# Sliding-window attention in blocks of 32 queries by 64 keys instead of 64 by 96, in a fused attention and mixture-of-experts kernel

## The chip, the core and the metric

The kernel runs on one core of a Trainium2 chip. The metric is the device time of one execution in microseconds (us). The kernel before takes 619.64 us, the median of three runs (619.24 to 620.0). "TensorE" is the matmul engine (PE in the profile, PEld its weight loads), "VectorE" is DVE, "ScalarE" ACT, "GpSimd" POOL, and SP issues most loads.

## The reference

Attention with a local window, then two feed-forward layers, all in fp32:

```python
q, k, v: (2, 8, 576, 64)            # batch, heads, positions, head size
rel = pos[:, None] - pos[None, :]
mask_plain = (rel >= 0) & (rel < 32)                      # heads 0 to 3
mask_dil = (rel >= 0) & (rel < 128) & (rel % 4 == 0)      # heads 4 to 7
scores = where(mask, q @ k.T / 8, -1e9)
attn = exp(scores - max); attn = attn / (attn.sum(-1) + 1e-9)
x = (attn @ v), heads side by side                        # (1152, 512)
p = domain_probs / (domain_probs.sum(-1) + 1e-9)
x = sum over 4 experts e of p[:, e] * (relu(x @ w1[e]) @ w2[e])   # 512 -> 1024 -> 512
h = x @ w_in                                              # 512 -> 2048
out = (h - tanh(h)) @ w_out
```

Each query sees 32 keys: in a plain head its own position and the 31 before it, in a dilated head every fourth position back. A dilated head is four plain windows over positions of equal remainder by 4.

## The kernel before

The 1152 tokens are worked in two sets: set 0 has the first 512, set 1 the other 640 (`SETS`). The feed-forward products ("dense products" below) are in fp32r, each value split into a high and a low part (`split`, line 761), so that every product is three matmuls; from the third weight slice on, a seven-product scheme (`PROD`, `product`) saves one product in eight. They stream 512, 320 or 256 columns.

Attention is worked in blocks of `BQ` = 64 queries by `BK` = 96 keys (64 and a halo of 32). Host code (`_pack`) lays q, k and v out by `PARTS`. The tensors q and k lie with the head size on the partitions, two heads above each other (a = 0, 1), and pairs of heads c = 0, 1. For set 0, class `Piece` works in two halves of 256 tokens, for the plain and the dilated heads; for set 1, class `Pair` works four times, once per kind and pair of heads.

1. Scores (lines 1096 and 1241): fp32 products with 64 partitions (head size) and 64 queries as weights, streaming 96 keys. They stand in a PSUM bank as stacks: 128 partitions (two blocks of 64 queries) by 96 columns per stack, four or five stacks in a bank.
2. Mask: in set 0 a bf16 product of an identity with a stored mask opens the bank, and the scores add to it (`open`, line 1230). In set 1 VectorE adds a stored mask (`masked`, line 1118).
3. Softmax (lines 1124 and 1278): maximum on VectorE, exponential on ScalarE, sum, reciprocal, and the division as a product on GpSimd. `STYLE` chooses, for a bank, one exponential per stack with its sum (0) or one for all (1).
4. Transposes (line 1155): TensorE turns each stack of 128 x 96 into 96 x 128, and ScalarE copies the bank to SBUF.
5. Value products (lines 1190 and 1319): v as weights (96 keys on the partitions, 64 columns), 64 queries streamed, two heads into the two halves of a bank's partitions. The result is x, which ScalarE copies out.

The short last blocks of the dilated heads of set 1 (16 positions) are 32 queries wide and have a stack of their own (`load_v_short`, `last`).

The order of all instructions is made by a planner, class `Order`: operations are recorded with assumed costs and dependencies, then laid out engine by engine. TensorE goes through a list; operations marked `fill` may be pulled forward into waits, and `idle` fillers (`warm`, products of zeros) are dropped where there is nothing to fill. `first_attention` (line 1770) writes the list for set 0, `when` gives due times for set 1. Loads go on SP's queue in the planned order, the first k pieces on ScalarE's.

All instructions are recorded through one helper, so the profile gives line 340 for nearly all; rows are told apart by their tiles: `x,x` are scores, `ident,att` transposes, `w,h`, `att,h` and `att,x` with 64 columns as weights are value products, `p` masks, `zero` fillers, and 128 x 128 forms of `x,w` and `w,h` dense products.

Of the kernel before, what the change touches and what calls it, by code (L numbers as in the profile page):

```python
# [25 lines left out]
BQ = 64  # L26
# [13 lines left out]
]  # L40
OF = {(0, True): [0], (0, False): [1, 2], (1, True): [3, 4], (1, False): [5, 6, 7, 8]}


def blocks(W, plain):

    M = BQ if plain else W
    return W * DIL // M, M, M + HALO


def _halves():  # L50

    out, at = [], [0, 0, 0]
    for part, plain in PARTS:
        out.append((part, plain, tuple(at)))
        nb, M, K = blocks(part[2], plain)
        at[0] += 2 * nb * M
        at[1] += 2 * ((nb - 1) * (M if plain else K) + K)
        at[2] += nb * 4 * HEAD
    return out, at
# [160 lines left out]
class Program:  # L220
# [69 lines left out]
    def group(self):  # L290
        return _Group(self)
# [6 lines left out]
def _joined(found):  # L298

    if len(found) < 4:  # L300
        return list(found)
    plain = [r for r in found]
    return [(
        min(r[0] for r in plain), max(r[1] for r in plain),
        min(r[2] for r in plain), max(r[3] for r in plain), None,
    )]


class _Group:

    def __init__(self, program):
        self.program = program

    def __enter__(self):
        self.program.open = [0.0, [], [], []]
# [8 lines left out]
class Engine:  # L324
# [22 lines left out]
    def cost(self, method, kw, outs, ins):  # L347
        n = math.prod(outs[0].shape[1:])
        psum = any(v.tile.ring.psum for v in (*outs, *ins))
        if self.name == "tensor":  # L350
# [3 lines left out]
            if kw["lhsT"].dtype == F32:  # L354
                return 0.055 if n == 96 else 0.071, False
# [3 lines left out]
        if self.name == "scalar":  # L359
            if "accum_out" in kw:  # L360
                return 0.335 if any(v.tile.ring.psum for v in ins) else 0.39, False
# [317 lines left out]
def tile_local_attention_moe_tanhshrink(  # L679
# [97 lines left out]
    NST = {0: 4, 1: 5}  # L777
    masks, spare = {}, {}
    for g in range(2):
        for p in (True, False)[:1 + g]:  # L780
            t = Tile(p_r, [128, 640], BF16, loose=True).view()
            masks[g, p], spare[g, p] = t[:, :NST[g] * BK], t[:, NST[g] * BK:]
    ident_bf = spare[0, True][:, :128]
# [6 lines left out]
    m_ = {}  # L790

    def cols(m, j, n, p=slice(0, 128)):
        return m[p, j * BK:(j + n) * BK].rearrange("p (n w) -> p n w", w=BK)

    def wide(m, n, p=slice(0, 128)):
        return m[p].unsqueeze(1).to_broadcast([p.stop - p.start, n, BK])

    def emit_consts():

        m = masks[0, True]  # L800
# [1188 lines left out]
```

## Time and profile before

| | |
|---|---|
| median of 3 runs | 619.64 us |
| profiled execution | 619.3 us, span 617.5 us |
| TensorE matmul, busy | 612.9 us (99%) |
| VectorE, ScalarE, GpSimd, busy | 375.2, 307.8, 317.7 us (61%, 50%, 51%) |
| chain that ended last | TensorE 98% |
| TensorE's granted clock | 0.999 of full speed |
| mean load and store rate | 110 GB/s, over 300 GB/s in the first 45 us |

The span is the time from the first to the last instruction; the execution's own time has 1.8 us more around it. Ends of matmuls are modelled, so neighbouring rows overlap; distances between starts are read instead where it matters. A row of the trace merges instructions of a kind: the start, the time to the last end, and the count.

### The profile page before, as it was taken

How to read it: one execution, taken by the hardware profiler on the slowest of the kernel's cores; microseconds unless marked ns; L12 is line 12 of the kernel's file. 1: busy time of each engine (PE TensorE's matmuls, PEld its weight loads, DVE VectorE, ACT ScalarE, POOL GpSimd, SP SyncE). 2: the span in 40 equal slices, each digit the busy share in tenths (PEclk: the TensorE clock that was granted, in tenths of full speed). 3: DMA queues.
4: the chain of work that ended last, by engine and by line, in shares of the span. 5: the costliest groups of instructions: out<-in, count | busy, mean ns of one | idle time of the engine just before them, and what ended most of it. 6: DMA issues, size and time to landing. Idle time of an engine off the chain costs nothing.

```text
span 617.5 us, 10655 instructions
## 1 busy us (share of the span) xinstructions
PE 612.9 (99%) x4034; PEld 542.4 (88%) x4034; DVE 375.2 (61%) x726; ACT 307.8 (50%) x743; POOL 317.7 (51%) x281
## 2 busy tenths in 40 slices
PE   9999999999999999999999999999999999999998
PEld 5887798989889889889889889898898988988986
DVE  5764566867766767755425454547786676653652
ACT  7886675654434434424314355344766553652440
POOL 4779873754345335335425459764755663461220
PEclk9999999999999999999999999999999999999999
DMA  8993144172444455312112112333105424300012
GB/s 303 359 323 108 36 135 124 52 243 98 139 138 167 137 176 181 103 69 69 35 34 69 35 34 70 124 94 111 66 1 171 120 86 136 103 2 1 17 52 85
DMA packets 37554, 68.03 MB, mean 110 GB/s; under 512 B 4224, under 2 KB 12032, under 8 KB 37504
## 3 DMA queue, kind: packets, MB, share of 16 engines
q1 hardware_dynamic: 37216, 67.07, 33.4%
q8 instruction: 31, 0.51, 0.3%
q10 hardware_dynamic: 288, 0.30, 0.2%
q14 instruction: 19, 0.16, 0.1%
HBM read 56.61 MB, written 10.75 MB: 109 GB/s over the span
## 4 chain that ended last, share of the span: by engine, by line
PE 98%; DVE 1%; ACT 0%; POOL 0%; issue 0%; DVEq 0%; POOLq 0%; ACTq 0%
PE bank L340 98%; DVE x L340 0%; ACT att L340 0%; DVE bank L340 0%; DVE st L340 0%; POOL att L340 0%; DVE acc L340 0%; DVE att L340 0%; DVE h L340 0%; DVE zero L340 0%; DVEq L340 0%; POOLq L340 0%; ACTq L340 0%
## 5 line engine op out<-in xcount | busy, mean ns | idle before, releaser
L340 PE MATMUL bank<-w,h 128*128 128x512 f32 (+2 forms) x1404 | 323.5, 383 | 0.0
L340 PE MATMUL bank<-x,w 128*128 128x256 f32 (+2 forms) x1992 | 287.7, 299 | 0.4 <-DVE bank L340 0.4
L340 PEld LDWEIGHTS bank<-x,w 128*128 128x128 f32 x1992 | 277.8, 188 | 10.8 <-DVE bank L340 0.6
L340 PEld LDWEIGHTS bank<-w,h 128*128 128x128 f32 (+1 forms) x1404 | 241.4, 185 | 49.7 <-ACT w L340 1.0
L340 POOL TENSOR_TENSOR w<-raw,w 128x512 fp32r<-128x512 f32 x102 | 135.8, 1343 | 144.8 <-ACT w L340 143.3
L340 ACT ACTIVATE h<-bank 128x320 fp32r<-128x320 f32 (+4 forms) x168 | 69.0, 422 | 79.7 <-PE bank L340 65.7
L340 DVE SCALAR_TENSOR_TENSOR acc<-bank,pn,acc 128x512 f32<-128x512 f32 x59 | 44.2, 750 | 74.6 <-PE bank L340 74.6
L340 DVE TENSOR_TENSOR bank<-bank,p 128x320 f32<-128x320 f32 (+1 forms) x132 | 61.3, 467 | 37.1 <-PE bank L340 24.1
L340 DVE SCALAR_TENSOR_TENSOR h<-bank,h 128x320 fp32r<-128x320 f32 (+2 forms) x124 | 56.1, 464 | 35.3 <-ACT h L340 34.4
L340 ACT ACTIVATE w<-raw 128x512 fp32r<-128x512 f32 x108 | 67.5, 628 | 18.0 <-PE bank L340 15.6
L340 DVE SCALAR_TENSOR_TENSOR att<-att 128x512 int32<-128x512 int32 (+1 forms) x96 | 73.1, 777 | 1.3
L340 ACT ACTIVATE p<-bank 128x320 f32<-128x320 f32 (+1 forms) x88 | 36.3, 413 | 63.6 <-PE bank L340 62.8
L340 POOL TENSOR_TENSOR w<-sum,w 128x512 fp32r<-128x512 f32 x36 | 47.6, 1322 | 38.3 <-ACT w L340 38.2
L340 ACT ACTIVATE att<-bank 128x256 f32<-128x256 f32 (+3 forms) x78 | 32.2, 430 | 50.1 <-PE bank L340 42.5
L340 DVE TENSOR_TENSOR acc<-bank,acc 128x512 f32<-128x512 f32 (+1 forms) x28 | 18.8, 671 | 34.4 <-PE bank L340 34.3
L340 POOL TENSOR_TENSOR h<-att,h 128x256 fp32r<-128x256 f32 (+1 forms) x28 | 22.8, 835 | 26.8 <-ACT h L340 26.1
L340 ACT ACTIVATE att<-att 128x512 f32<-128x512 f32 (+2 forms) x39 | 25.3, 658 | 22.7 <-DVE att L340 16.9
L340 ACT ACTIVATE w<-sum 128x512 fp32r<-128x512 f32 x36 | 22.6, 628 | 20.5 <-PE bank L340 19.7
L340 POOL TENSOR_TENSOR sum<-raw 128x512 f32<-128x512 f32 x12 | 16.1, 1341 | 31.9 <-DMA raw<-in_moe_w_dram 17.8
L340 POOL TENSOR_TENSOR att<-att,st 128x480 f32<-128x480 f32 (+1 forms) x20 | 19.1, 956 | 14.2 <-DVE st L340 11.6
L340 DVE TENSOR_TENSOR bank<-bank,att 128x256 f32<-128x256 f32 (+1 forms) x32 | 14.8, 463 | 9.4 <-ACT att L340 9.1
L340 ACT ACTIVATE acc<-bank 128x512 f32<-128x512 f32 (+4 forms) x27 | 12.9, 505 | 11.7 <-PE bank L340 11.2
(73 smaller groups left out, 352.6 us busy)
## 6 DMA issues: line engine op xcount, KB each, us to landing
raw<-in_moe_w_dram SPq DMA_DIRECT2D x40, 512.0 KB, 3.9
att<-in_moe_w_in_dram SPq DMA_DIRECT2D x16, 512.0 KB, 5.0
att<-in_moe_w_out_dram SPq DMA_DIRECT2D x16, 512.0 KB, 4.9
in<-att SPq DMA_DIRECT2D x16, 256.0 KB, 3.8
out<-att SPq DMA_DIRECT2D x16, 256.0 KB, 3.3
raw<-in SPq DMA_DIRECT2D x8, 512.0 KB, 4.2
raw<-out SPq DMA_DIRECT2D x8, 512.0 KB, 3.7
h<-in_v_dram SPq DMA_DIRECT2D x7, 512.0 KB, 7.4
```

What stands on the lines that cost most here:

```text
L340: getattr(self.engine, method)(**real)
```

## The change

Blocks become 32 queries by 64 keys (`BQ` = 32). A score product has 32 query columns as weights and streams 64 keys; four blocks of 32 stand above each other and the two heads' rows of the array are used at once, so there are eight places in the array for it. A stack is 128 x 64, two stacks (s = 0, 1) are turned by one transpose of 128 x 128, and afterwards their keys lie on partitions 0 to 63 and 64 to 127. Value products are 64 keys deep and stream 32 queries; the two stacks use the two halves of the partitions and go to two banks, the two heads to the halves of a bank. So v is loaded with 128 partitions, the rows of one block above those of another. `Pair` and `Piece` become `Part` and `Early`: one softmax bank now holds both pairs of heads. Masks are made on TensorE from a small 64-row tile (`near`, `pick_`, `mask_in`). Rows of tokens in set 0 come in another order, which `y_sum` undoes. Planned costs and due times change with it.

The diff, cut to its core:

```diff
-BQ = 64
+BQ = 32
 BK = BQ + HALO
...
+    def mask_in(b, p, n, first):
+        m = 2 * first * BK
+        with P.group():
+            for to, x in ((b[:, :m], near), (b[:, m:n * BK], near[:, BK:])):
+                if to.shape[1]:
+                    w = x.shape[1]
+                    pe.matmul(
+                        out=to.rearrange("p (n w) -> p n w", w=w), lhsT=pick_[p],
+                        rhs=x.unsqueeze(1).to_broadcast([64, to.shape[1] // w, w]),
+                        start=True, stop=False, skip_group_check=True,
+                    )
...
     def emit_masks():
-        std, first = m_["std"], m_["first"]
...
+        for p in (True, False):
+            b = bank()
+            mask_in(b, p, 6, 2 if p else 1)
+            copy(masks[p], b[:, :6 * BK])
...
-            nb, M, K, n, at = self.parts[0]
-            o = c * nb * M + half * 256
-            load(self.q[:, o:o + 256], q[:, at[0] + o:at[0] + o + 256])
-            a, b = (0, 3 * M + K) if half == 0 else (3 * M + K, n)
-            load(self.k[c][:, a:b], k[:, at[1] + c * n + a:at[1] + c * n + b], queue)
+        def load_piece(self, c, u, queue="sync"):
+            at = HALVES[0][2]
+            for to, src, n in (
+                (self.home()[:, 512 * u + 256 * c:512 * u + 256 * c + 256], q[:, at[0] + 512 * c + 128 * u:], 128),
+                (self.home(c)[:, 320 * u:320 * u + 320], k[:, at[1] + 544 * c + 128 * u:], 160),
+            ):
+                load(
+                    to.rearrange("p (n w) -> p n w", n=2),
+                    src[:, :512].rearrange("p (n w) -> p n w", n=2)[:, :, :n],
+                    queue if n == 160 else "sync",
+                )
...
         def load_k_half(self, u):
-            t = self.k[u] = plain32(x_tile(self.g))
-            _, _, _, n, at = self.parts[u]
+            at, n = (HALVES[5][2][1], 1024) if u == 0 else (HALVES[4][2][1], 512)
...
+        def scores(self, c=None):
...
                     for a in range(2):
+                        r = slice(D * a, D * a + D)
+                        o = (2 * j + s) * BK
                         pe.matmul(
-                            out=self.sb[a][part:part + qs.shape[1], j * BK:(j + 1) * BK],
-                            lhsT=qs[D * a:D * a + D, :], rhs=ks[D * a:D * a + D, :],
-                            start=True, stop=True,
+                            out=self.sb[a][BQ * i:BQ * i + BQ, o:o + BK],
+                            lhsT=self.h.q[r, qo:qo + BQ], rhs=self.h.k[kt][r, ko:ko + BK],
+                            start=not opened_, stop=True, skip_group_check=True,
                         )
...
+            n = self.n * BK
             with P.group():
-                for j in range(4):
+                for j in range(0, n, 128):
                     pe.transpose(
-                        out=pb[:BK, j * 128:(j + 1) * 128], in_=t[:, 0, j * BK:(j + 1) * BK],
-                        identity=ident,
+                        out=pb[:, j:j + 128], in_=t[:, 0, j:j + 128], identity=ident,
                     )
...
+            banks = [bank() for _ in range(2)]
...
+                for j, s, i, i0, n, vt, vo, c, o, step in self.valued:
+                    rows = slice(64 * s, 64 * s + 64)
+                    w = j * 128 + BQ * i + i0
                     for a in range(2):
-                        f0 = j * 4 * D + (2 * self.c + a) * D
...
+                        f0 = vo * 4 * D + (2 * c + a) * D
+                        to = banks[s][D * a:D * a + D]
...
                         pe.matmul(
-                            out=to, lhsT=h.v[tile_][:BK, f0:f0 + D], rhs=w, start=True, stop=True,
+                            out=to, lhsT=h.v[vt][rows, f0:f0 + D], rhs=self.pt[a][rows, w:w + n],
+                            start=True, stop=True, skip_group_check=True,
                         )
```

How TensorE's list moves. Its beginning before, from the last filler ahead of the first scores (`zero` are fillers, `p` is the mask tile, `x,x` are scores):

```order
L340 LDWEIGHTS zero
L340 MATMUL bank<-zero 32x512
L340 LDWEIGHTS p
L340 MATMUL bank<-p 128x384
L340 MATMUL bank<-x_71,x_69 64x96 x8
```

Five more fillers stand ahead of these rows. The beginning now, from the first row:

```order
L362 LDWEIGHTS p
L362 MATMUL bank<-p 128x256
L362 LDWEIGHTS p
L362 MATMUL bank<-p 128x128
...
L362 LDWEIGHTS zero
L362 MATMUL bank<-zero 32x512
...
L362 MATMUL bank<-x_69,x_67 32x64 x16
L362 MATMUL bank<-x_83,x_67 32x64 x16
```

The list begins with masks, one filler is left ahead of the scores, and both pairs of heads are scored in a row.

TensorE's list around the first dense product, before (`x,w` is dense, `w,h` with 64 x 64 are values):

```order
L340 MATMUL bank<-ident,att 96x128 x4
L340 MATMUL bank<-w_311,h_176 64x64 x8
L340 LDWEIGHTS zero
L340 MATMUL bank<-zero 32x512
L340 MATMUL bank<-w_311,h_176 64x64 x8
L340 LDWEIGHTS p
L340 MATMUL bank<-p 128x384
L340 LDWEIGHTS p
L340 MATMUL bank<-p 128x384
L340 MATMUL bank<-x_327,w_331 128x256
```

And now:

```order
L362 MATMUL bank<-w_247,h_172 64x32 x32
L362 LDWEIGHTS p
L362 MATMUL bank<-p 128x256
L362 LDWEIGHTS p
L362 MATMUL bank<-p 128x256
L362 MATMUL bank<-ident,att 128x128 x4
L362 MATMUL bank<-x_396,w_390 128x256
L362 MATMUL bank<-x_433,w_390 128x256
```

All 32 value products of the first dilated half stand in one group, and four transposes of the second half have come ahead of the first dense product.

## Rows read from the trace of the kernel before

**Rows 1.** The page, part 4: the chain that ended last, by engine.

```profile
PE 98%; DVE 1%; ACT 0%; POOL 0%; issue 0%; DVEq 0%; POOLq 0%; ACTq 0%
```

**Rows 2.** The chain in order of time: start us, us, what.

```profile
9.32 443.19 PE bank L340 x3022
...
457.26 157.28 PE bank L340 x906
```

**Rows 3.** TensorE's groups, 16.42 to 103 us: shapes xcount | busy us, mean ns.

```profile
L340 PE MATMUL bank<-w,h 128*128 128x512 f32 x136 | 35.1, 402 | 0.0
L340 PE MATMUL bank<-x,w 128*128 128x256 f32 x180 | 24.5, 287 | 0.0
L340 PE MATMUL bank<-x,w 128*128 128x512 f32 x48 | 12.1, 401 | 0.0
```

**Rows 4.** TensorE's timeline, dense products alone: start us, us, what, count.

```profile
117.96 2.95 PE L340 MATMUL bank<-w,h 128*128 128x512 f32 x12
120.75 0.87 PE L340 MATMUL bank<-x,w 128*128 128x256 f32 x6
121.46 2.95 PE L340 MATMUL bank<-w,h 128*128 128x512 f32 x12
```

**Rows 5.** The same, scores and values with dense products beside them.

```profile
17.36 0.56 PE L340 MATMUL bank<-x,x 64*64 64x96 f32 x16
...
29.82 1.15 PE L340 MATMUL bank<-att,h 96*64 96x64 f32 x32
...
33.80 2.99 PE L340 MATMUL bank<-x,w 128*128 128x256 f32 x24
36.73 1.06 PE L340 MATMUL bank<-x,x 64*64 64x96 f32 x40
37.71 3.10 PE L340 MATMUL bank<-x,w 128*128 128x256 f32 x24
40.65 1.56 PE L340 MATMUL bank<-w,h 128*128 128x512 f32 x6
...
63.93 0.80 PE L340 MATMUL bank<-att,h 96*64 96x64 f32 x20
```

**Rows 6.** The same, transposes among dense products.

```profile
53.00 0.60 PE L340 MATMUL bank<-ident,att 128*96 128x128 f32 x4
53.35 3.03 PE L340 MATMUL bank<-x,w 128*128 128x512 f32 x12
56.22 0.82 PE L340 MATMUL bank<-ident,att 128*96 128x128 f32 x6
```

**Rows 7.** Windows at the short scores: us, PE busy (x counted), PEclk, DMA share, GB/s.

```profile
61.31:61.32 0.00, 0.00 (x4) 1.00 0.00 0
61.31:61.37 0.06, 0.06 (x12) 1.00 0.00 0
```

**Rows 8.** TensorE's timeline, short value products (32 columns) and the next row.

```profile
101.04 0.49 PE L340 MATMUL bank<-att,x 96*64 96x32 f32 x12
101.36 0.67 PE L340 MATMUL bank<-att,h 96*64 96x64 f32 x16
```

**Rows 9.** All engines' timeline: the first weights on VectorE and GpSimd.

```profile
13.36 0.83 DVE L340 CAST w<-raw 128x512 fp32r<-128x512 f32 x1
...
14.28 1.28 POOL L340 TENSOR_TENSOR w<-raw,w 128x512 fp32r<-128x512 f32 x1 [0.36 <-DVE w L340]
```

**Rows 10.** A window of the first loads: busy by engine, PEclk, DMA share, GB/s.

```profile
3.00:4.00 1.00, 1.00 (x3) 0.10 (x1) 0.00 (x0) 0.91 (x3) 0.86 (x6) 1.00 1.09 346
```

**Rows 11.** TensorE's timeline, the first two groups of scores.

```profile
4.05 1.53 PE L340 MATMUL bank<-x,x 64*64 64x96 f32 x16
...
6.10 0.88 PE L340 MATMUL bank<-x,x 64*64 64x96 f32 x16
```

**Rows 12.** ScalarE's groups, 6.4 to 16.1 us: shapes xcount | busy us, mean ns | idle.

```profile
L340 ACT ACTIVATE att<-bank,st 128x96 f32<-128x96 f32 x16 | 5.2, 341 | 1.5 <-DVE st L340 1.3
...
L340 ACT ACTIVATE x<-bank 128x256 fp32r<-128x256 f32 x3 | 1.1, 378 | 0.1
```

More of the change, by code (lines that the diff above doesn't have):

```diff
@@ L54, in _halves @@
         out.append((part, plain, tuple(at)))
[L55 to L58, printed above, removed]
+        W = part[2]
+        at[0] += 2 * DIL * W
+        at[1] += 2 * (DIL * W + HALO if plain else DIL * (W + HALO))
+        at[2] += blocks(W, plain)[0] * 4 * HEAD
     return out, at
@@ L288, in op, with group @@
         self.ops.append(o)
-    def group(self):
-        return _Group(self)
+    def group(self, begin=0.0):
+        return _Group(self, begin)
 def _covers(a, b):
@@ L818, in emit_consts @@
[L818 to L844 removed]
+        dve.memset(ap=near[BQ:, :HALO], constant=NEG)
@@ new lines, in take @@
+        def take(self, s, b):
+            u = self.u
+            if self.h.plain:
+                n = 2 if u else 3
+                x = xall[1][:, :2, 384 * u:384 * u + 128 * n].rearrange(
+                    "p c (n s w) -> p c n s w", n=n, s=2
+                )[:, :, :, s if u else 1 - s]
+                copy(x, b[:, :128 * n].rearrange("p (c n w) -> p c n w", c=2, n=n))
+                return
+            x = xf[1][2 + u]
+            copy(x[:, 64 + 256 * s:320 + 256 * s], b[:, :256])
+            for i in range(2):
+                copy(
+                    x[:, 576 * i:576 * i + 64].rearrange("p (n s) -> p n s", s=2)[:, :, s],
+                    b[:, 256 + 32 * i:288 + 32 * i],
+                )
@@ new lines, in x_home, with begin, cold, number @@
+                xall[g] = sum_tile(g).rearrange("p (k n) -> p k n", k=KD)
+                xf[g] = [xall[g][:, kk] for kk in range(KD)]
+    class Early(Part):
+        def begin(self):
+            for a in range(2):
+                b = self.sb[a] = bank()
+                mask_in(b, self.h.plain, 4, 0 if self.u else 2)
+        def cold(self):
+            return self.u in COLD
+        def number(self, a):
+            return 4 * self.u + 2 * (not self.h.plain) + a
+        def style(self, a):
+            n = self.number(a)
@@ L1767, in tile_local_attention_moe_tanhshrink, with part @@
     kinds = {(g, p): Kind(g, p) for g in range(2) for p in (True, False)}
-    both = [Piece(kinds[0, p]) for p in (True, False)]
+    early = [[Early(kinds[0, p], u) for p in (True, False)] for u in range(2)]
     def first_attention():
-        def score(half, i, *cs):
-            for c in cs or (0, 1):
-                both[i].scores(half, c)
+        def part(k):
+            return early[k // 4][k % 4 // 2]
         def soft(*ks):
             for k in ks:
-                both[k % 4 // 2].softmax((k // 4, k % 2))
+                part(k).softmax(k % 2)
         def turn(*ks):
             for k in ks:
-                both[k % 4 // 2].transposes((k // 4, k % 2))
-        def use(half, i, c):
-            both[i].values(half, c)
+                part(k).transposes(k % 2)
         def fill(*todo):
```

624 lines of the change are left out of this document (256 added, 368 removed), and 6 rows, old and new, of the table PARTS.

## The prediction

> **What bounds the kernel now.** Read the chain of waits on the page first: TensorE has 98% of it [rows 1]. Then the same chain in order of time: two pieces, of 443.19 and 157.28 us, are TensorE matmul after matmul, and only for 4.7 us between them does the chain pass through other engines [rows 2]. So from 9.32 us on, everything that TensorE is handed costs its own length, and work on other engines costs nothing while they keep up. The change does not touch the dense products (the order lists hold the same 3300 before and after). What it changes is how long attention occupies TensorE between them, and how soon they can begin.
>
> Attention stands between dense products from 16.42 us to about 103 us. That stretch of 86.58 us holds 136 + 48 dense products of 512 columns and 180 of 256 [rows 3]. A dense product costs, from row start to row start where nothing else stands between, (120.75 - 117.96) / 12 = 0.2325 us with 512 columns and (121.46 - 120.75) / 6 = 0.118 us with 256 [rows 4]. The dense part is 184 x 0.2325 + 180 x 0.118 = 64.0 us, so **attention has 22.6 us of the path** there. Before 16.42 us it hides behind loads and softmax, and is counted separately below.
>
> **What a group of small products costs.** An fp32 product in the order list is two instructions in the trace (136 + 16 scores against 272 + 32), so counts below are the trace's. Scores run four at a time: 40 are busy for 1.06 us and 16 for 0.56 [rows 5], 0.083 us for each round of four and 0.23 fixed. The dense products on both sides show what a group takes from the path: from 33.80 to 40.65 us lie 48 dense products of 256 columns (5.66 us) and the 40 scores [rows 5], leaving 1.19, which is 0.13 above the busy time. Fixed cost of a group on the path: 0.36 us. Value products run two at a time: 32 in 1.15, 20 in 0.80 [rows 5] give 0.058 us a pair and 0.22 fixed, 0.36 with the same 0.13. Transposes: 6 take 0.82 and 4 take 0.60, 0.11 each; the dense row starts 0.35 after the four begin [rows 6], and the first interval of such a dense run is about 0.1 longer, so a group costs its count x 0.11 and next to nothing more.
>
> **Scores.** Each now has 32 query columns in the array and streams 64 keys instead of 96, eight at a time, in twice the number. That eight can run at once is shown already: at the short scores (32 wide) eight new starts fall into 0.05 us [rows 7]: four older ones are still counted when the window opens, twelve at its end. For the price of a round I bound it: 0.055 us if it shrinks with the columns (0.083 x 64 / 96), 0.083 if it does not shrink. I take 0.058, near the lower end, because a value product of 64 columns has just that interval. After 16.42 us there will be five score groups: 64, 64 and three of 96, so 52 rounds: 52 x 0.058 + 5 x 0.36 = 4.8 us.
>
> **Values.** The sums are 64 deep, so four products run at once, but each carries 32 queries instead of 64, and there are twice as many. Halving the columns should halve a round; the rows say no. Twelve short products with 32 columns, two at a time, take 0.32 us to the next row [rows 8], 0.053 a pair, against 0.058 with 64 columns. Something other than the stream sets that pace, and loading the weights (64 columns in either case) is what stays the same. So I charge 0.058 for a round of four: three groups of 64 and three of 96 are 120 rounds, 120 x 0.058 + 6 x 0.36 = 9.1 us. The round count of before is the same 120; only the fixed costs shrink. Bounds of the round: 0.053 and as much above, 0.6 us either way.
>
> **Transposes.** A stack is 128 wide in place of 96 and holds two blocks. 56 transposes after 16.42 us become 26, of which four stand ahead of the first dense product: 22 or 26 x 0.11 = 2.4 to 2.9 us, against 56 x 0.11 = 6.2 before. This is the largest term.
>
> Sum: 4.8 + 9.1 + 2.9 = 16.8 in place of 22.6, or with the four hidden 16.4. **Gain about 5.7 us**.
>
> **The start.** Here the change pays back. The first dense product needs weights: raw data are cast by VectorE at 13.36 (0.83 us) and completed by GpSimd from 14.28 (1.28) [rows 9], so at 15.6; TensorE arrives at 16.42 after the values. Ahead of those weights in the load queue come now, in KB, 4 x 128 + 4 x 160 for the plain blocks in place of 544 + 512, and 2 x 256 dilated k in place of 2 x 192: 224 KB more. At 346 GB/s [rows 10] that is 0.65 us. The plain pieces are cut in rows of 512 and 640 bytes instead of 1024 and 1152; the trace has no load so cut at the start, so I bound it by 0 and by their whole time again at two thirds of that rate (1152 KB: 1.7 us), and take 0.4, nearer to the former because the rows that are added, the dilated k, are 2 KB long. Weights: ready near 16.7.
>
> The softmax chain also moves. A first stack now needs both head pairs' loads, 0.6 us later than the first pair alone, and TensorE, which before had six filler products ahead of its first score, must now build masks from the identity first: its first row is a mask, and one filler remains. The first 16 scores of before took 1.53 us and the next 16 took 0.88 [rows 11], twice the spacing, though the granted clock reads 1.00 [rows 10]: by their spacing the first ones ran at the lower of the two levels. The later start keeps all 64 there. So ScalarE's first exponential moves from 6.48 to about 7.2. Its list up to the first dense product: 16 exponentials at 0.34 less some 0.03 for 64 columns instead of 96, four copies of transposed stacks, now 256 columns at 0.38 like those of x [rows 12], two exponentials of the second half at about as much, four copies of x at 0.38: 4.9 + 1.5 + 0.8 + 1.5 = 8.7 us, to 15.9, and about 0.8 of waits for GpSimd's last product and TensorE's turn. After the last stack copy near 15.7 stand 64 value products (16 x 0.058 + 0.36 = 1.3) and four transposes (0.45) ahead of the first dense product: 17.4. I take **17.3, 0.9 us later**; bounds: 16.4 (no loss) and 18.8 (the slow load and the late chain add up).
>
> VectorE, ScalarE and GpSimd have less to do per stack (256 or 384 columns in place of 384 or 480), so I charge them nothing afterwards: they keep up now with longer stacks, or the long pieces of [rows 2] would have breaks. If that cover failed, TensorE would wait for the transposed stacks or for x.
>
> Total: 619.3 of the profiled execution (span 617.5 and 1.8 around it) less 5.7 plus 0.9 = 614.5. The median of the runs is 0.3 above the profiled one: **614.9 us**, 0.8% faster.
>
> **A rule that speaks against the change.** The rows show starts of small products 0.007 us apart, eight in a round [rows 7]. The Trainium skill, "TensorEngine Tiling (Array Packing)", section "Instruction Overhead", says that each matmul has an overhead of about 60 cycles and warns against taking a tiling factor from a dimension that is already small; "TensorE: Matmul & The Clock Gate", section "Wait — 56ns, not 53.3ns?", puts the least distance of two starts at about 25 ns. By that floor (an estimate from these pages) 896 small products would need 22.4 us instead of 10 and the kernel would be near 627. The eight starts in 0.05 us contradict it for products in different tiles.
>
> **Rivals.** (1) An instruction floor. If small products cannot follow each other faster, on average, than four-tile rounds show now (0.083 / 4 = 0.0206 us), the 416 score and 480 value instructions after the first dense product cost 18.5 us instead of 52 x 0.058 + 120 x 0.058 = 10.0: 8.5 more, **623.4, slower**. It decides from 0.0163 us on, where the gain of 4.7 is gone. Against it: [rows 7]. For it: only sixteen such products were ever in a row. (2) A starved start: loads in small rows and an idle TensorE. If the first dense product comes at 18.8 and the clock is then still at its lower level for some 4 us (as it was from 0.94 to about 5), 1.5 and 2 us are lost: **618.4**, the edge of no change. For it: no filler can stand ahead of the masks. Against: the order list puts 22 fillers into the later gaps. (3) Halved value rounds: if the 64-deep rounds go by columns, 0.029, 120 x 0.029 = 3.5 us more are gained: **611.4**. Against it: [rows 8].
>
> **How the numbers follow.** Forecast 0.78, floor 0.06, starved start 0.11, halved rounds 0.05. A measurement of this kernel tells apart some 0.2%, 1.2 us. The forecast's own bounds: rounds -0.8 to +1.9, start -0.9 to +1.5, rarely all together: 612.8 to 617.8. With part of rivals 2 and 3 the range is **612.5 to 618.3**. Faster: the forecast, halved rounds and a little of the starved start, 0.86; within 0.2%: 0.08; slower: 0.06.
>
> **What would show it.** Groups of 64 scores busy about 0.70 us and of 96 about 0.93; 64 values 1.15 and 96 values 1.61; 38 transposes; the first dense product near 17.3; TensorE without waits after it; the first 320-column product some 4.5 to 5 us earlier. Score starts 0.02 apart, or dense products at double spacing near 17 us, would prove me wrong.

## The result, and the profile after

| | before | after |
|---|---|---|
| median, us | 619.44 (4 runs, 619.07 to 620.0) | 625.81 (4 runs, 624.96 to 626.86) |
| profiled execution, its span | 619.3, 617.5 | 625.26, 623.4 |
| first dense product | 16.42 | 21.32 (forecast 17.3) |

The ratio is 1.0105, 95% interval 1.009 to 1.0119: **slower by 1%**, where 614.9 us, 0.8% faster, had been forecast. The time lies outside the range.

The page after, in order the engines' row of part 1, the granted clock in 40 slices (part 2), the queue that carries instructions (part 3), and part 4 as in [rows 1]:

```profile
PE 613.4 (98%) x4625; PEld 541.7 (87%) x4625; DVE 374.0 (60%) x731; ACT 298.7 (48%) x743; POOL 308.4 (49%) x271
PEclk9899999999999999999999999999999999999999
q8 instruction: 36, 0.59, 0.4%
PE 97%; DVE 1%; issue 1%; ACT 0%; POOL 0%; POOLq 0%; DVEq 0%
```

"issue" has grown from 0% to 1%, and the clock dips near the start. The queue of instructions moved 36 packets; 4625 products and as many weight loads are 257 instructions a packet. The kernel before, the same two parts of its page:

```profile
PE 612.9 (99%) x4034; PEld 542.4 (88%) x4034; DVE 375.2 (61%) x726; ACT 307.8 (50%) x743; POOL 317.7 (51%) x281
q8 instruction: 31, 0.51, 0.3%
```

The chain in order of time, after, beside [rows 2] (start us, us, what):

```profile
13.60 0.39 issue
13.98 4.58 PE bank L362 x126
18.57 1.66 issue
20.23 46.63 PE bank L362 x721
66.86 1.42 issue
...
91.85 366.11 PE bank L362 x2292
```

Three times TensorE stands still for nothing that the profile shows. Counted over all its records in the trace (products, weight loads and its own waits for semaphores), 449, 705 and 2241 stand ahead of the ones that come late: 193, and one, two and eight times 256 more. All three waits stand where a block of 256 instructions ends. In the kernel before, TensorE has no such wait; its shortest block is this one (us, PE, PEld, DVE, ACT, POOL, PEclk, DMA share, GB/s):

```profile
10.13:18.19 8.06, 8.06 (x139) 5.84 (x131) 6.83 (x19) 7.07 (x27) 6.03 (x6) 1.00 1.03 392
```

Where the forecast's terms went (TensorE's timeline, worked out from starts as in the prediction):

| term | forecast, us | measured, us |
|---|---|---|
| first dense product | 17.3 | 21.32 |
| five score groups behind it | 4.8 | 9.25: rounds of 0.100 (2.1 more), wait at 66.86 (1.6), low clock at 23.66 (0.7) |
| six value groups | 9.1 | 9.8, 0.8 of it a wait for banks at 91 us |
| 26 transposes | 2.9 | 3.0 |
| dense products at double spacing, 21 to 25 us | 0 | 0.9 |

The rows add up to 10.2 us more than forecast; 10.8 lie between 614.5 and 625.26. By starts of rows alone it is 9.7: the first product of 320 columns comes at 109.83 us, forecast for 100.1 (104.93 before, plus 0.9, less 5.7). From the first dense product to there it takes 88.51 us before and after alike, so behind the first dense product nothing was won. Another 1.0 us lies behind 109.83, most of it spread evenly over dense products that both kernels share; the control run before_dense below has 0.9 there too, so it is not put down to the change. TensorE's timeline at the start, products only (start us, us, operation, count, wait before it):

```profile
4.77 1.46 PE L362 MATMUL bank<-x,x 64*32 64x64 f32 x64
...
6.70 2.88 PE L362 MATMUL bank<-zero 128*32 128x512 bf16 x9
9.51 1.01 PE L362 MATMUL bank<-x,x 64*32 64x64 f32 x64
...
13.98 1.25 PE L362 MATMUL bank<-zero 128*32 128x512 bf16 x5 [0.39 <-issue]
15.17 1.14 PE L362 MATMUL bank<-w,h 64*64 64x32 f32 x64
...
17.57 1.00 PE L362 MATMUL bank<-w,h 64*64 64x32 f32 x50
20.23 0.43 PE L362 MATMUL bank<-w,h 64*64 64x32 f32 x14 [1.66 <-issue]
...
21.32 2.41 PE L362 MATMUL bank<-x,w 128*128 128x256 f32 x12
```

Nine fillers hold the dilated scores until 9.51, four of them at double spacing. The dilated values break off after 50 of 64, and the first twelve dense products then take 2.41 us. Windows of the same stretch (us, PE, PEld, DVE, ACT, POOL, PEclk, DMA share, GB/s):

```profile
13.98:20.23 6.25, 4.58 (x126) 2.94 (x127) 3.43 (x14) 2.83 (x10) 4.91 (x6) 1.00 1.06 399
64.85:68.28 3.43, 2.01 (x143) 1.81 (x135) 0.57 (x1) 2.91 (x7) 2.99 (x3) 1.00 0.03 5
22.00:23.00 1.00, 1.00 (x7) 1.00 (x6) 0.75 (x3) 1.00 (x3) 0.51 (x1) 0.50 1.13 305
24.00:25.00 1.00, 1.00 (x62) 0.89 (x44) 0.00 (x0) 0.00 (x0) 1.00 (x1) 0.50 0.60 161
```

The first two windows are the blocks of 256 instructions whose successor came late: 6.25 us while loads ran at 399 GB/s, 3.43 while almost nothing else moved. (The one from 9.59 to 13.98, with the wait of 0.39 at its end, lasted 4.39 us at 359 GB/s.) In the last two the granted clock is at 1.2 of 2.4 GHz; it fell near 21.9 us, behind the wait of 1.66, and was back by 25.4. The queue of instructions in two windows, 17.5 to 18.8 and 65.4 to 67.1 us (packets, MB, share of 16 engines):

```profile
q8 instruction: 1, 0.02, 5.1%
q8 instruction: 1, 0.02, 5.2%
```

In each, one packet: 0.051 x 16 x 1.3 = 1.06 and 0.052 x 16 x 1.7 = 1.41 us long. TensorE goes on 1.3 to 1.5 us after it ends. What differs, by the packets' starts in the trace, is how long the packet takes to begin: 3.73 us from the block's first instruction under the loads, 0.70 with the queues almost empty.

So theory 1 was formed: **TensorE's instructions come in blocks of 256, one block is fetched while the one before it runs, and small products use a block up sooner than the next one comes.** The Trainium skill, "Runtime: NRT & Kernel Launch", section "Instruction fetch mechanics", describes refills of 256 instructions over a queue of the sequencer's own, fetched while the block before runs. By that the trace agrees (257 instructions a packet, one packet in each of the two windows). It calls the cost mostly hidden, because instructions are dispatched more slowly than blocks are filled; here the two windows above speak against it.

### The profile page after: what moved, and what is told of

It is laid out like the page before. It is cut to its first block, busy times and chain, and to the rows that moved or that the text cites. A ratio compares the mean times of both kernels' runs of the same rounds, so it can differ in the third digit from the quotient of the medians.

```text
span 623.4 us, 11837 instructions
## 1 busy us (share of the span) xinstructions
PE 613.4 (98%) x4625; PEld 541.7 (87%) x4625; DVE 374.0 (60%) x731; ACT 298.7 (48%) x743; POOL 308.4 (49%) x271
## 4 chain that ended last, share of the span: by engine, by line
PE 97%; DVE 1%; issue 1%; ACT 0%; POOL 0%; POOLq 0%; DVEq 0%
PE bank L362 97%; DVE x L362 0%; DVE bank L362 0%; DVE h L362 0%; ACT h L362 0%; DVE p L362 0%; POOL p L362 0%; ACT att L362 0%; DVE acc L362 0%; DVE att L362 0%; POOLq L362 0%; POOLq masks.py:199 0%; DVEq L362 0%; POOLq L1915 0%
## 5 line engine op out<-in xcount | busy, mean ns | idle before, releaser
L362 PEld LDWEIGHTS bank<-x,w 128*128 128x128 f32 x1992 | 278.6, 189 | 10.8 <-DVE bank L362 0.7
L362 POOL TENSOR_TENSOR w<-raw,w 128x512 fp32r<-128x512 f32 x102 | 133.7, 1325 | 146.6 <-ACT w L362 140.6
L362 DVE SCALAR_TENSOR_TENSOR att<-att 128x512 int32<-128x512 int32 (+1 forms) x96 | 75.6, 807 | 1.6 <-ACT att L362 0.3
L362 ACT ACTIVATE p<-bank 128x320 f32<-128x320 f32 (+2 forms) x90 | 37.1, 414 | 54.1 <-PE bank L362 53.5
L362 ACT ACTIVATE att<-bank 128x256 f32<-128x256 f32 (+2 forms) x72 | 28.8, 414 | 49.6 <-PE bank L362 42.0
L362 DVE TENSOR_TENSOR acc<-bank,acc 128x512 f32<-128x512 f32 (+1 forms) x28 | 18.8, 672 | 34.5 <-PE bank L362 34.4
L362 ACT ACTIVATE att<-att 128x512 f32<-128x512 f32 (+2 forms) x39 | 24.6, 639 | 22.1 <-DVE att L362 14.1
L362 ACT ACTIVATE w<-sum 128x512 fp32r<-128x512 f32 x36 | 22.6, 628 | 20.8 <-PE bank L362 20.1
L362 POOL TENSOR_TENSOR att<-att,st 128x256 f32<-128x256 f32 (+1 forms) x20 | 14.5, 726 | 19.7 <-DVE st L362 15.6
L362 DVE TENSOR_SCALAR att<-att 128x512 int32<-128x512 int32 x32 | 16.3, 515 | 4.6 <-DMA out<-att 2.3
```

The lines of the kernel that those rows point to most:

```text
L362: getattr(self.engine, method)(**real)
```

## The experiments

**The order of the score products.**

```diff
-for c_, j, s, i, qo, kt, ko in self.scored:
+for c_, j, s, i, qo, kt, ko in sorted(self.scored, key=lambda x: x[1:4]):
```

> The changed kernel with its score products in another order, nothing else: the places of the array are walked through with the stack outermost, so that eight products in a row stand in eight different places; in the changed kernel the two stacks of one place follow right after one another, and its starts come in pairs (0.0066 us apart, then 0.020). Theory 1 (the order makes the round): the starts of a round come closer together, 64 scores are busy about 0.70 us instead of 1.02, 96 about 0.93 instead of 1.34 or more; five groups after the first dense product give back 5 x 0.3 to 0.35 and some more, the time falls by 1.5 to 2.1 us, to about 623.5. Rival (the instruction floor of the prediction, 0.0125 us for an instruction whatever its place): no change of the busy times, 0 us. Should the faster groups run into the end of a block of 256 instructions, an 'issue' wait after them takes some of the gain back.

624.31 us, 1.0086 (1.0072 to 1.01). TensorE's timeline after, then with the edit, 96 and 64 scores:

```profile
41.06 1.41 PE L362 MATMUL bank<-x,x 64*32 64x64 f32 x96
53.79 1.01 PE L362 MATMUL bank<-x,x 64*32 64x64 f32 x64
```

```profile
41.16 1.17 PE L362 MATMUL bank<-x,x 64*32 64x64 f32 x96
53.66 0.86 PE L362 MATMUL bank<-x,x 64*32 64x64 f32 x64
```

The order matters, half as much as expected. By the medians 1.5 us are won; the interval overlaps that of the change (1.009 to 1.0119), so it is the timeline that shows it: a round of eight falls from 0.100 to 0.080 us (96 scores start within 0.954 instead of 1.191 us), not to 0.058. The waits stay (issue 4.0 us in four pieces).

**Values and scores of set 1 apart.**

```diff
-        when(due, begin)
+        when(due + 3.0 * (n > 1), begin)
```

> The changed kernel with the third and fourth score group of set 1 due 3 us later, so that dense products stand between the values and the scores that follow one another at 64 to 68 us. Theory 1 (TensorE's instructions come in blocks of 256, the next block is asked for when one is begun and takes 3.4 us or more, so 96 values and 96 scores in a row, 384 instructions in 2.6 us, outrun it): the 'issue' wait of 1.42 us before the last five scores is gone and no other comes in its place, the time falls by about 1.4 us to 624.2 or so. Rival (the wait belongs to the scores, for instance their operands or banks): the wait moves along with the scores, the time stays within 0.4 us.

624.15 us, 1.0078 (1.0065 to 1.0092). The timeline now, without a wait:

```profile
66.55 1.60 PE L362 MATMUL bank<-att,h 64*64 64x32 f32 x96
68.08 2.36 PE L362 MATMUL bank<-w,h 128*128 128x512 f32 x9
70.37 1.44 PE L362 MATMUL bank<-x,x 64*32 64x64 f32 x96
```

The wait at 64 to 68 us is gone, as theory 1 had it: 1.7 us less by the medians, with intervals that just overlap. That no other comes in its place does not hold for the profiled execution, the slowest of the five (626.22 us). Its start came late by a load, and it has a wait that the change had not, with 961 records ahead of it (193 and three times 256 more):

```profile
27.48 0.78 PE L362 MATMUL bank<-w,h 64*64 64x32 f32 x39 [1.36 <-issue]
```

**No fillers behind the first scores.**

```diff
-            if self.cold():
-                warm(pb, 12)
...
-            if self.cold():
-                warm(banks[0], 12)
...
-        warm(idle, 6)
...
-        warm(idle, 12)
```

> The changed kernel without the fillers that stand behind the first scores (products of zeros that only keep TensorE busy); one filler ahead of the scores stays. Theory 1 (the fillers, planned at 0.213 us each and running at 0.3 to 0.43 while the clock is at its lower level, hold back the dilated scores from about 8 to 9.51 us and the plain values from 14.3 to 15.17, and their 40 instructions bring the next block's end nearer): dilated scores start 1 to 1.8 us earlier, the first dense product comes at 19 to 20 us instead of 21.32, the time falls by 1 to 2 us if the clock rises all the same. Rival (the fillers keep the clock up): scores, values and dense products run at double spacing for longer, the granted clock reads 0.5 over more than 6 us after 10 us, and the time rises by 1 to 3 us. Second rival (the loads set the start): the dilated scores still start at 9 us or later, no change.

621.44 us, 1.0032 (1.002 to 1.0045), far more won than any of the three had expected, and not where theory 1 looked. Its timeline:

```profile
6.65 1.46 PE L362 MATMUL bank<-x,x 64*32 64x64 f32 x64
...
18.56 0.60 PE L362 MATMUL bank<-p 64*128 64x256 bf16 x2
...
21.53 3.75 PE L362 MATMUL bank<-x,w 128*128 128x256 f32 x18
...
63.16 1.60 PE L362 MATMUL bank<-att,h 64*64 64x32 f32 x96
64.69 1.41 PE L362 MATMUL bank<-x,x 64*32 64x64 f32 x96
```

The dilated scores start 2.9 us earlier, everything up to about 24.6 us goes at double spacing, as the first rival had said, if not with its time (dense products start 0.213 us apart, then 0.118), and still the first dense product comes only 0.2 us later: ahead of it TensorE has been through 819 instructions, with the next scores among them, instead of 735. No issue wait is left. (A view shows the granted clock as 1.00 up to 24.6 us too, but the trace has no record of it there: the first begins at 24.58, where the spacing halves, in the change at 8.28 and in the kernel before at 5.42.) And 96 values and 96 scores stand as close as before, without a wait between: with fewer instructions ahead, the ends of the blocks fall elsewhere. The wait belongs to a place in the count, not to the scores.

**Dense work ahead of the dilated values.** `whole` is cut in its two halves (`only`), of which the first needs the plain heads' x alone; the casts of the first weights (`w1_all`) are planned there too.

```diff
+        ready["w1"] = 0
+        w1_all(0)
+        for f in range(2):
+            whole(0, f, 0, 0)
         early[0][1].values()
...
```

> The changed kernel with the plain half of the first two dense steps (12 products, which need only the plain heads' x and the first weights) put ahead of the dilated values on TensorE's list. Theory 1 (the 'issue' wait of 1.66 us at 18.57 is a wait for the next block of instructions, 256 after the one at 13.98): a dense product costs as many instructions as a value but ten times as long, so it fills that wait; TensorE's issue wait there is 0.3 us or less, the clock does not fall to its lower level at 22 us, and 1.5 to 3.5 us are won. Rival (the weights are not there before 18.6 us, since VectorE casts them behind the softmax): TensorE waits for w instead, 1 us or more, ahead of the first dense product; the clock falls as before and less than 1 us is won.

622.24 us, 1.0044 (1.0032 to 1.0057): 3.6 us won.

```profile
17.91 1.67 PE L362 MATMUL bank<-x,w 128*128 128x256 f32 x12
19.50 1.43 PE L362 MATMUL bank<-w,h 64*64 64x32 f32 x64
```

The dense products lie over the fetch; the 64 values behind them lose 0.3 us and the clock stays at its upper level. TensorE does not wait for weights here. The other wait, with 2241 records ahead, stays: 1.04 us at 65.14.

**A burst in the kernel before, and the same spread out.** `tiny(n)` is a group of n products of zeros, 64 x 32 weights and 32 columns; the output is not touched.

```diff
...
+    for i in range(1):          # spread: range(6)
+        when(110.0 + 4.0 * i, lambda: tiny(384))          # spread: tiny(64)
```

> The kernel before, with its large blocks, and 384 tiny products of zeros (64 x 32 weights, 32 columns, eight places of the array in turn, results unused) put in one group among dense products well behind attention: 768 instructions in a row that need no data. Theory 1 (instructions come in blocks of 256; the next is asked for when one is begun, and arrives 3.1 to 3.4 us later at this place): two 'issue' waits inside the group, 256 instructions apart, each 3.1 to 3.4 us less the time of 256 instructions (1.3 to 3 us), so 0.3 to 2.1 us each; the time rises by these beside the products' own 2 to 5 us. Rival (a wait of TensorE for operands or banks, or a floor for each instruction): the starts inside the group go on evenly to its end, no gap above 0.2 us.

> The same 384 tiny products in the kernel before, but in six groups of 64 with at least 4 us of dense products between. Theory 1: no 'issue' wait at all, although the instructions and their order within a group are the same; each group takes its own 0.4 to 0.8 us and about 0.36 fixed, so against the kernel before with one group only the fixed cost is more (5 x 0.36 = 1.8 us) and the two waits are gone. Rival (a floor for each instruction): the starts inside a group are as far apart as in the one group's parts between waits, and the sums differ by the fixed costs only.

632.49 us, 1.0217 (1.0196 to 1.0238), for the burst and 625.63, 1.0107 (1.0093 to 1.0121), spread. The burst on TensorE's timeline:

```profile
163.22 1.71 PE L340 MATMUL bank<-zero 64*32 64x32 bf16 x190
167.40 1.20 PE L340 MATMUL bank<-zero 64*32 64x32 bf16 x128 [2.47 <-issue]
172.22 0.70 PE L340 MATMUL bank<-zero 64*32 64x32 bf16 x66 [3.62 <-issue]
```

Two waits, exactly 128 products, which are 256 instructions, apart, in products that need no data and in a kernel that had no such wait. The block takes 1.2 us to run, and the next comes after 3.71 and 4.82 us (starts of 167.40 and 172.22, and 163.69 for the first), so the waits are longer than the 0.3 to 2.1 us expected. Between waits the products start 0.008 us apart, so no floor explains this. Two windows of the burst:

```profile
163.69:167.40 3.71, 1.24 (x150) 1.15 (x139) 3.64 (x7) 0.91 (x2) 0.00 (x0) 1.00 0.26 96
167.40:172.22 4.82, 1.20 (x128) 1.10 (x128) 0.27 (x1) 0.00 (x0) 0.00 (x0) 0.57 0.79 226
```

The second also has the clock at its lower level, which goes on to 178.3 us and is part of the 13 us lost. Spread, one wait came that theory 1 had not expected:

```profile
178.65 0.50 PE L340 MATMUL bank<-x,w 128*128 128x256 f32 x2
180.14 0.75 PE L340 MATMUL bank<-x,w 128*128 128x256 f32 x4 [0.99 <-issue]
```

It stands in dense products, behind a group: the block begun at 173.86 was used up in 5.3 us, and its successor took 6.28. So even one group of 64 in four microseconds can be too dense. How long a block takes to come was foretold in neither run. The packets tell which part varies: those of the burst begin 1.17 and 1.62 us behind the block's first instruction, the one of the spread run 3.97, with less traffic in its block than in the second window of the burst (188 GB/s against 226).

**Edits together.** The order of scores, the groups apart, and the dense halves; in the second run `warm(idle, 12)` becomes `warm(idle, 3)`.

> Three edits together in the changed kernel: the scores' order by places, the later score groups of set 1, and the dense half steps ahead of the dilated values. If the causes are independent as theory 1 has it, the gains add: 1.3 to 1.5 (order), 1.4 to 1.7 (apart), 3.4 to 3.6 (dense), together 6 to 6.5 us from 625.8: 619.2 to 619.8, level with the kernel before. Rival (one cause, a late start that everything waits for, whichever edit mends it): less than 4.5 us together, 621.3 or more.

> As the run before it, and the group of twelve fillers ahead of the dilated scores cut to three. Theory 1 with the fillers holding the dilated scores: these start at 7.5 to 8 us instead of 9.5 to 10.2, the dense products at 16.5 to 17.5 instead of 17.9, and 0.5 to 1.5 us more are won: 618 to 619. Rival (the fillers bring the clock up, and the run without them kept double spacing until about 23 us): with three of them the products from 8 us on still go at double spacing, and the time is the same as without this edit or up to 1.5 us more.

620.26 us, 1.0016 (1.0008 to 1.0025): 5.6 us less than the change alone, where the three gains by themselves make 6.7. So they add but for 1.2 us; the time misses the expected 619.2 to 619.8 and stays well below the rival's 621.3. With three fillers 620.62, 1.0021 (1.0011 to 1.003), a miss: the dilated scores start at 7.80 and the dense products at 16.46, a microsecond earlier. Double spacing lasts to 13.2 us instead of 9.3, as the rival had said, and a wait for instructions takes the gain back:

```profile
18.69 0.89 PE L362 MATMUL bank<-w,h 64*64 64x32 f32 x45
20.57 0.53 PE L362 MATMUL bank<-w,h 64*64 64x32 f32 x19 [1.00 <-issue]
```

**More dense work ahead, and a control.** Four and three half steps instead of two, with the weights `a21` cast second; the control makes the edit of two half steps in the kernel before.

```diff
-            for name in ("a11", "a12", "a21", "a22"):
+            for name in ("a11", "a21", "a12", "a22"):
...
-        for f in range(2):
+        for f in range(NF):          # combo3_few: range(3)
```

> As the run with three edits together, but all four plain half steps (24 products, first weights alone, whose second half is cast right after the first) stand ahead of the dilated values, not two. Theory 1: 2.8 us of dense work with only 48 instructions lie over the wait for the next block, which is then in before the values need it; no 'issue' wait in the first 35 us; against that run 0 to 0.7 us less, 619.5 to 620.3. Rival (the second half of the weights comes 1.3 us after the first, so TensorE waits for w): a wait for w of 0.3 to 1.3 us between the twelfth and the thirteenth product, the time the same or up to 0.5 us more.

> The same with three fillers instead of twelve ahead of the dilated scores. Theory 1: the 1.00 us 'issue' wait inside the dilated values of the earlier run with three fillers is gone, first dense product at 16.5 or a little before, 0.5 to 1 us less than there: 619.6 to 620.1. Rival (the wait only moves behind the dense products): an 'issue' wait of 0.5 us or more at another multiple of 256 instructions within the first 35 us, no gain.

> The same with three half steps ahead (18 products) and the fourth step whole behind. Theory 1: between the runs with two and with four; the block arrives about 6.3 us after the one before it was begun while the loads run at 300 GB/s and more, so 18 products cover all but 0.3 us of the wait: 619.7 to 620.4. Rival as before: no gain over two half steps.

> A control: the kernel before, large blocks, with the one edit that did most for the changed kernel (two plain half steps ahead of the dilated values). Theory 1 (the edit covers the wait for instructions, of which the kernel before has none at its start): a first dense product up to 0.5 us earlier but no more than 0.5 us won in all, 618.7 to 619.5. Rival (the edit helps any kernel, since it gives TensorE dense work in an idle stretch): 1.5 us or more are won, 617.6 or less, and the kernel before stays ahead of every version of the changed one.

| run | us | ratio (95% interval) | first dense | issue waits, us |
|---|---|---|---|---|
| combo4 | 619.93 | 1.001 (1.0002 to 1.0019) | 17.18 | none by this name; 1.05 at a block's end |
| combo4_few | 621.53 | 1.003 (1.0021 to 1.0039) | 16.20 | 2.5, longest 1.9 |
| combo3_few | 620.58 | 1.0018 (1.0009 to 1.0028) | 16.22 | 3.1, longest 1.9 |
| before_dense | 621.39 | 1.0032 (1.002 to 1.0045) | 15.86 | none |

The expected "no wait in the first 35 us" fails for combo4, although its page lists no "issue": the row with 449 records ahead is late there too, under another name.

```profile
14.49 0.81 PE L362 MATMUL bank<-zero 128*32 128x512 bf16 x3 [1.07 <-PE bank L362]
```

With fewer fillers the rival came true: whatever starts earlier runs into the next block's end. For combo4_few that is 24 us:

```profile
23.99 0.43 PE L362 MATMUL bank<-w,h 64*64 64x32 f32 x15
26.31 1.35 PE L362 MATMUL bank<-w,h 64*64 64x32 f32 x49 [1.90 <-issue]
```

The control got slower, by some 2 us, which neither side had expected: its dense products come 0.56 us earlier, but TensorE has no wait for instructions there that they could cover. Its first product of 320 columns comes 0.55 us later than before (105.48), and 0.9 lie behind that. Why it loses was not followed up.

**The instructions without the work.** 128 tiny products behind the first half's scores in the kernel before.

```diff
         score(0, 1, 1)
+        tiny(128)          # in the run its lines stand here in full
         soft(2, 3)
```

> The kernel before with 128 tiny products of zeros (256 instructions, about 1 us of work, results unused) put into its start, behind the scores of the first half, where TensorE otherwise idles or runs fillers. Ahead of its first dense product it then has 645 TensorE instructions instead of 389; the changed kernel has 735. Theory 1 (under the first loads a block of 256 instructions comes about every 6 us, and this sets the changed kernel's start): one 'issue' wait of 1.5 to 4 us ahead of the first values, the first dense product 1.5 to 4 us later than 16.42, the time 1.5 to 4 us more. Rival (loads, softmax and fillers set the start): the tiny products vanish in the idle stretch, no 'issue' wait, the time within 1 us.

625.83 us, 1.0089 (1.0072 to 1.0105): 256 instructions of no use, put where TensorE had time, cost the kernel before about as much as the change does. The size was underestimated; timeline and two windows of the profiled execution, the slowest of six (622.74 to 626.51 us), tell why:

```profile
10.89 0.39 PE L340 MATMUL bank<-x,x 64*64 64x96 f32 x7
14.47 0.63 PE L340 MATMUL bank<-x,x 64*64 64x96 f32 x9 [3.19 <-issue]
...
23.04 1.64 PE L340 MATMUL bank<-x,w 128*128 128x256 f32 x6
```

```profile
7.90:14.47 6.57, 2.95 (x146) 2.21 (x146) 3.05 (x12) 4.72 (x25) 3.30 (x4) 0.98 1.01 357
15.00:16.00 1.00, 1.00 (x20) 0.93 (x16) 0.00 (x0) 0.00 (x0) 0.00 (x0) 0.50 1.05 418
```

The block begun at 7.90 lasts 6.57 us, under loads of 357 GB/s. TensorE stands still for 3.19 us of it, the clock falls to its lower level at its end and stays there until about 24.5 us, and so the first dense product comes 6.6 us late, not 1.5 to 4.

**Two waits for banks.** Three half steps with twelve fillers (combo3) and four half steps (combo4b), and in both the values of the second part of set 1 a step later.

```diff
-        when(due + LATER + 13.8, part.values)
+        when(due + LATER + 13.8 + 1.5 * (n == 1), part.values)
```

> The changed kernel with the scores' order by places, the later score groups, three plain half steps ahead of the dilated values with twelve fillers as at first, and the values of the second part of set 1 one step (1.5 us) later. Theory 1: three half steps leave a bank free, so that the next scores' masks do not wait for VectorE (0.96 us with four half steps); the 0.8 us wait of the values near 86 us for banks goes with the shift. Both together 1 to 1.8 us less than with four half steps: 618.2 to 619, below the kernel before by up to 0.2%. Rival (the start is bounded by the supply of instructions whatever their order): an 'issue' wait of 0.5 to 1.5 us in the dilated values comes back, 619.5 or more.

> The version with four plain half steps, and only the values of the second part of set 1 shifted by a step (1.5 us). Theory 1: their wait near 86 us for banks (0.8 us, by VectorE's h) is gone, 0.6 to 0.9 us less than without the shift: 619.0 to 619.3, level with the kernel before. Rival (the wait moves with them): no change, 619.9.

combo3: 620.33 us, 1.0017 (1.0008 to 1.0025). The rival: waits of 0.17 and 0.96 us for instructions at 20.1 and 25.4 us. combo4b: **619.51 us, 1.0003 (0.9995 to 1.0012)**, level with the kernel before. Its first dense product came at 16.12, a microsecond earlier than in combo4: the wait of 1.05 us there is missing here, with the same instructions up to that point, since the packet began 1.66 instead of 2.53 us behind the block's first instruction. So the 0.4 us cannot be put down to the shift. No version tried beats the kernel before.

## Why the prediction was wrong, step by step

**"From 9.32 us on, everything that TensorE is handed costs its own length."** This is the step that failed. It holds for the kernel before, whose whole blocks of 256 instructions all last 8.06 us or more, and so it was read there without a break. The change turns 389 instructions ahead of the first dense product into 735, and 384 into one place at 64 to 67 us. The sum priced products by rounds and had no term for the instructions' own way to the engine. No rival had it either. What the runs show in its place: three waits for instructions of 3.5 us together, and 1.6 us for what then ran at the lower clock (0.7 and 0.9 in the table), 5.1 of the 10.8 us missed. burst and before_tiny show the cause without the change, dense, apart and the shift of the wait in nofill show it inside. And the place fits throughout: in fourteen of the traces, of either kernel, TensorE stands still for more than 0.1 us with 449, 705, 961, 2241, 3265 or 3521 records ahead, 24 times in all, and each time goes on 1.2 to 1.6 us after a packet of the instruction queue has ended.

**The start, 17.3 forecast, 21.32 measured.** The chain was followed rightly at its beginning: first exponential 7.18 us against 7.2, load rates as before (346 GB/s at 3 to 4 us in both). (That the first scores ran at the lower level was rightly read from their spacing; the 1.00 of [rows 10] is no measurement, since the trace has no record of the clock before 5.42 us.) Then it failed in three places: nine fillers, four of them at half speed, hold the dilated scores to 9.51, as the prediction had not asked what the plan's fillers do at the lower clock; the block's end holds the plain values (0.39) and the dilated ones (1.66); and the clock falls behind that. With dense work over the fetch the first dense product came at 16.12 to 17.91, near the forecast's value, but with 64 values moved behind it, so this alone does not bring the forecast's time. Runs that started earlier met a wait further on (combo_few, combo3, combo4_few). That the supply of instructions bounds the whole start, in whatever order, is suggested by them and not shown: dense got through its block from 10.29 to 13.66 in 3.37 us, under loads of 375 GB/s, without a wait.

**Scores, 0.058 us a round, in truth 0.100, and 0.080 in a better order.** A term mis-sized: five groups cost 2.1 us more, 1.1 in the better order. The value 0.058 was taken from a value product of 64 columns; but 0.058 there is for four products, and eight in a round do not start in the time of four. What sets 0.080 was not settled. The row "eight new starts in 0.05 us" [rows 7] said that places can overlap, not that a long run of them keeps the pace.

**Values and transposes.** Right: four values in 0.058 us, 64 in 1.28 us of path; 38 transposes in all, of which the 26 behind the first dense product take 2.99 us, the 56 before 6.5. Without the waits and at the upper clock, attention behind the first dense product would be 5.9 + 9.0 + 3.0 = 17.9 us (an estimate from these rows, scores as in the order run; 18.9 with those of the change) against the 16.8 forecast and 22.6 before. The mechanism was right; by this estimate it is worth 4.7 us, 3.7 as the change stands. No run delivered it whole.

**Rivals.** (1) The floor gave 623.4, nearest to the outcome, by another cause: small products follow each other 0.0125 us apart in the changed kernel, 0.0100 in the better order and 0.008 in the burst, all below the 0.0163 from which it would decide. (2) The starved start had the right symptoms (18.8 and a low clock for 4 us; measured 21.32 and 3.4 us), but named loads and fillers, and gave 618.4. (3) Halved value rounds: did not happen.

**The rule weighed in the prediction.** The Trainium skill's least distance of two starts, about 25 ns in "TensorE: Matmul & The Clock Gate", section "Wait — 56ns, not 53.3ns?", gave about 627 there, close to the 625.26 measured. The nearness is chance. The trace does not agree with the rule: 0.008 us in the burst.

## What to carry to other kernels

Count instructions where products are small: here blocks of 256 instructions that ended in a wait lasted 3.1 to 3.4 us among the dense products near 65 us and 4.4 to 6.8 while loads ran at 350 to 410 GB/s, so 384 instructions in 2.6 us made a wait when a whole block lay among them. A wait that stands at a fixed count of TensorE's records (here 193 and a multiple of 256), whatever its name, and that shifts when unrelated instructions ahead are added or taken out, is the sign; long products laid between, not an earlier start, were the cure here. Splitting work into finer blocks saves array time and pays for it in instructions; both belong in the sum.

## What the runs showed of the hardware that was not expected

- Blocks of 256 TensorE instructions that ended in a wait lasted 3.08 (dense) and 3.43 us (after) at 5 GB/s of traffic, 3.71 (96), 4.82 (226), 4.39 (359), 6.25 (399) and 6.57 (357); but 6.28 at 188 GB/s in the spread run, so the rate alone does not tell it. In 24 such waits the packet of the instruction queue began 0.6 to 5.3 us behind the block's first instruction, took 0.9 to 1.8 us, and TensorE went on 1.2 to 1.6 us after its end; so it is mainly the packet's own wait that varies.
- Products of 32 columns in eight places in turn start 0.0075 (spread) to 0.008 us (burst) apart on average; scores that come twice in a row to the same place (after) start 0.007 and 0.020 us apart in turn at first, and a run of 96 of them takes 1.191 us of starts instead of 0.954 (order).
- At the end of waits of 1.36 (apart), 1.66 (after, order), 1.90 (combo4_few), 2.47 (burst) and 3.19 us (before_tiny), or up to 1.9 us behind them, the granted clock fell to its lower level, for 3.4 us in the first four runs and 10.2 us in the last two; behind one of 1.92 in combo3_few it did not. What decides was not tried.
- In the first microseconds of a run products stand at double spacing. The trace has no record of the granted clock there, though views show 1.00; its first record begins where the spacing halves, at 5.42 us (before), 8.28 (after), 13.20 (combo_few) and, without fillers, 24.58 (nofill).
